# Second-half values turned by the DMA crossbar instead of TensorE, and a fixed table for the units between the feed-forward steps

## The chip, the cores and the metric

The kernel runs on one core of one Trainium2 chip. The metric is the device time of one execution in microseconds (us). A trace of the hardware profiler goes with one execution of each kernel; its span runs from the first to the last recorded instruction and is 1.7 to 2.2 us shorter than the device time, which matters below. Kernels of one job ran on the same chip, in turn with the kernel before.

## The reference

Attention with block-sorted keys and values, then a bilinear feed-forward layer. Cut to what matters:

```python
B, H, S, D = 4, 8, 768, 64;  n_blocks = 8          # blocks of 96 positions
P = sort_net                                        # (B, H, 8, 8), five rounds of
                                                    # exp and row and column normalisation
k_sorted = einsum('bhij,bhjcd->bhicd', P, k_blocks) # mix blocks of k, and of v
v_sorted = einsum('bhij,bhjcd->bhicd', P, v_blocks)
attn = softmax(q_blocks @ k_sorted^T / 8)           # within each block of 96
x = (attn @ v_sorted), heads side by side           # (3072, 512)
out = ((x @ w_a) * (x @ w_b)) @ w_out               # w_a, w_b: 512x1536, w_out: 1536x512
```

## The kernel before

(PSUM, in what follows, is the memory into which TensorE writes its results; a semaphore is a counter on which an engine or a transfer queue waits; the DMA crossbar is what transposes a tile while a DMA transfer moves it.)

Everything is computed with heads in pairs (hp = 0 to 3 in the first batch). The first batch is the special one: nothing is there yet to hide its attention behind, so its positions are split into two halves of four blocks. The first half's attention runs ahead of all feed-forward work; the second half's is cut into units that stand between the twelve feed-forward steps of the first half.

The units that the change touches (cut):

```python
def half_scores(h, hp):              # "sc": scores of four blocks, then the exponential on ScalarE
    ...
    nc.scalar.activation(out=eT[:, 0, :, 0:HB], in_=sc[0:BLK, :, 0:HB], func=AF.Exp, ...)

def half_v(h, hp):                   # "vs_ps": v of four blocks turned by TensorE, copied by VectorE
    g = h * HP + hp
    vT, vs = vTs[hp], vss[g % NBUF]  # three buffers for turned v
    vs_ps = psF.tile([P, NBH, 2, D], BF16, tag="F", name="vs_ps")
    for i in range(NBH):
        nc.tensor.matmul(vs_ps[:, i], lhsT=vT[:, h * NBH + i], rhs=ident, is_transpose=True)
    nc.vector.tensor_copy(out=vs[0:BLK, 0:NBH, V0:V0 + P], in_=...vs_ps...)

def half_o(h, hp):                   # "o_ps": probabilities times v; reciprocal and scaling on VectorE
    ...
def half_x(h, hp, eng):              # "xt_ps": result turned by TensorE and copied into xT
    ...
```

and their order:

```python
def units_half():
    def R(hp):
        half_scores(1, hp)
        half_v(1, hp)
    us = []
    for hp in range(HP):
        us.append(lambda hp=hp: R(hp))
        if hp > 0:
            us.append(lambda hp=hp: half_x(1, hp - 1, "dve"))
        us.append(lambda hp=hp: half_o(1, hp))
    us.append(lambda: half_x(1, HP - 1, "dve"))
    return us

interleave(steps, units_half(), 1, 2)   # evenly: from the third step on, the last step alone
```

A step (`ffn_ab`) is eight matmuls of 128x384 into two PSUM tiles; steps are numbered from 0 to 11. GpSimd's queue loads k, v, q and the weights, in six chunks of w_a and w_b each; a chunk serves two steps. Later batches already have v turned by the crossbar (`return_v`).

The softmax here doesn't subtract the row's maximum and nothing guards it: scores larger than these inputs give would overflow.

Of the kernel before, what the change touches and what calls it, by code (L numbers as in the profile page):

```python
# [16 lines left out]
def _ap(t: bass.AP, extra_offset, pattern):  # L17
    return bass.AP(tensor=t.tensor, offset=t.offset + extra_offset,
                   ap=[list(p) for p in pattern])
# [3 lines left out]
def kernel(  # L23
# [11 lines left out]
    nc = tc.nc  # L35
    P = 128
# [10 lines left out]
    HP = H // 2  # L47
    KA = DMODEL // P
    KO = DFF // P
    NBH = NB // 2  # L50
# [4 lines left out]
    V0 = 16  # L55
# [18 lines left out]
    ident = const.tile([P, P], BF16, name="ident")  # L74
# [50 lines left out]
    NBUF = 3  # L125
    kTs = [const.tile([P, S + PAD], BF16, name=f"kT{n}") for n in range(HP)]
    vTs = [const.tile([P, NB, P], BF16, name=f"vT{n}") for n in range(HP)]
    eTs = [const.tile([BLK, 2, 2, HB + PAD], BF16, name=f"eT{n}") for n in range(NBUF)]
    vss = [const.tile([P, NB, VW], BF16, name=f"vs{n}") for n in range(NBUF)]
# [13 lines left out]
    def xT_of(b):  # L143
        if b not in xTs:
            xTs[b] = xtp.tile([P, KA, S], BF16, tag="xT", name="xT")
        return xTs[b]
# [12 lines left out]
    def copy(eng, out, in_):  # L159
        if eng == "act":  # L160
            nc.scalar.copy(out=out, in_=in_)  # L161
        else:
            nc.vector.tensor_copy(out=out, in_=in_)  # L163

    def keep_busy(ps, n, cols=512):
        for _ in range(n):
            nc.tensor.matmul(ps[:, 0:cols], lhsT=warm[:, 0:P], rhs=warm[:, 0:cols],  # L167
                             start=True, stop=True)


    def mix_mms(g, what, where):
        src2 = loaded[g][0 if what == "k" else 1]
        for c in range(NCH):
            for e in range(2):
                nc.tensor.matmul(where(c)[e * D:(e + 1) * D], lhsT=src2[:, e, c * D:(c + 1) * D],  # L175
                                 rhs=s_all[:, 2 * g + e], start=True, stop=True)

    def mix_first(g, what, engines, fill=0, cols=512):
        mix = [psF.tile([P, 512], FP32, tag="F", name="mixf") for _ in range(2)]
        keep_busy(mix[0], fill, cols)  # L180
        mix_mms(g, what, lambda c: mix[c // 3][:, c % 3 * P:(c % 3 + 1) * P])
        for u, eng in enumerate(engines):
            copy(eng, turned(g, what, u),
                 _ap(mix[u], 0, [[512, P], [P, 3], [CG, NB], [1, CG]]))

    def turned(g, what, u):
        if what == "k":
            return _ap(kTs[g % HP], u * 3 * CG, [[S + PAD, P], [CG, 3], [BLK, NB], [1, CG]])
        return _ap(vTs[g % HP], u * 3 * CG, [[NB * P, P], [CG, 3], [P, NB], [1, CG]])

    def half_scores(h, hp):
        g = h * HP + hp
        kT, qT, eT = kTs[hp], st[hp, "qT"], eTs[g % NBUF]
        sc = psA.tile([P, 2, 512], FP32, tag="A", name="sc")
        for i in range(NBH):
            for e in range(2):
                nc.tensor.matmul(  # L197
                    sc[:, e, i * BLK:(i + 1) * BLK],
                    lhsT=kT[e * D:(e + 1) * D, (h * NBH + i) * BLK:(h * NBH + i) * BLK + P],
                    rhs=qT[e * D:(e + 1) * D, :, (h * NBH + i) * CG:(h * NBH + i + 1) * CG],  # L200
                    start=True, stop=True)
        nc.scalar.activation(out=eT[:, 0, :, 0:HB], in_=sc[0:BLK, :, 0:HB],  # L202
                             func=AF.Exp, scale=float(scale))

    def half_v(h, hp):
        g = h * HP + hp
        vT, vs = vTs[hp], vss[g % NBUF]
        vs_ps = psF.tile([P, NBH, 2, D], BF16, tag="F", name="vs_ps")
        for i in range(NBH):
            nc.tensor.matmul(vs_ps[:, i], lhsT=vT[:, h * NBH + i], rhs=ident, is_transpose=True)  # L210
        nc.vector.tensor_copy(out=vs[0:BLK, 0:NBH, V0:V0 + P],
                              in_=vs_ps[0:BLK].rearrange("p i e d -> p i (e d)"))

    def half_o(h, hp):
        g = h * HP + hp
        xp = att.tile([BLK, NBH, 2, D], BF16, tag="xph", name="xph")
        one_o(eTs[g % NBUF], 0, vss[g % NBUF], 0, xp, NBH)
        st["x", h, hp] = xp

    def half_x(h, hp, eng):  # L220
        xT, xp = xT_of(0), st["x", h, hp]
        xt_ps = psF.tile([P, NBH, BLK], BF16, tag="F", name="xt_ps")
        for i in range(NBH):
            nc.tensor.matmul(xt_ps[:, i, :], lhsT=xp[:, i],  # L224
                             rhs=ident[0:BLK, 0:BLK], is_transpose=True)
        copy(eng, xT[:, hp, h * HW:(h + 1) * HW].rearrange("p (i t) -> p i t", i=NBH), xt_ps)

    def one_o(eT, hf, vs, i0, xp, nxp):
        rec = att.tile([BLK, 2, NBH], FP32, tag="rec", name="rec")
        o_ps = psA.tile([P, 2, 512], FP32, tag="A", name="o_ps")  # L230
        for i in range(NBH):
            for e in range(2):
                nc.tensor.matmul(o_ps[:, e, i * (D + 1):(i + 1) * (D + 1)],  # L233
                                 lhsT=eT[:, hf, e, i * BLK:i * BLK + P],
                                 rhs=vs[0:BLK, i0 + i, V0 - 1 + e * (D + 1):V0 + D + e * (D + 1)],
                                 start=True, stop=True)
        nc.vector.reciprocal(
            out=rec, in_=_ap(o_ps, 0, [[1024, BLK], [512 + D, 2], [D + 1, NBH]]))
        nc.vector.tensor_tensor(  # L239
            out=_ap(xp, i0 * 2 * D, [[nxp * 2 * D, BLK], [D, 2], [2 * D, NBH], [1, D]]),  # L240
            in0=_ap(o_ps, 1, [[1024, BLK], [511, 2], [D + 1, NBH], [1, D]]),
            in1=_ap(rec, 0, [[2 * NBH, BLK], [NBH, 2], [1, NBH], [0, D]]),
            op=ALU.mult)
# [180 lines left out]
    with tc.manual_schedule(engines={ET.PE, ET.Pool, ET.SP}):  # L424
        with tc.manual_schedule(engines={ET.Activation, ET.DVE}):
# [7 lines left out]
            for it in range(5):  # L433
# [8 lines left out]
                if it == 2:  # L442
                    with nc.allow_low_precision("sum of one one and zeros"):
                        nc.vector.reduce_sum(
                            out=mask, in_=_ap(ident, 0, [[P, P], [1, CG], [CG, NB]]),
# [14 lines left out]
                else:  # L460
                    nc.vector.tensor_mul(
                        out=p_fin.bitcast(BF16).rearrange("h (i j u) -> h i j u", i=NB, j=NB),
# [30 lines left out]
            def partial(n, *kcs):  # L493
                if n not in begun:
                    begun[n] = (psF.tile([P, 512], FP32, tag="F", name="pf") if n < 3 else
                                psA.tile([P, 2, 512], FP32, tag="A", name="two")[:, 0])
                ab_mms(begun[n], (w_a_sb, w_b_sb)[n % 2], 0, n // 2, 0, kcs)
# [3 lines left out]
            mix_first(1, "v", ("act", "dve"), 1)  # L501
            mix_first(1, "k", ("act", "dve"))
            half_scores(0, 0)
            half_v(0, 0)
            mix_first(2, "v", ("act", "dve"))
            mix_first(2, "k", ("act", "act"))
            half_o(0, 0)
            half_scores(0, 1)
            half_v(0, 1)
            half_v(0, 2)  # L510
            mix_first(3, "k", ("dve", "act"))
            half_scores(0, 2)
            half_o(0, 1)
            mix_first(3, "v", ("act", "act"))
            half_x(0, 0, "dve")
            half_o(0, 2)
            half_x(0, 1, "act")
            half_scores(0, 3)
            partial(0, 0)
            half_v(0, 3)  # L520
            partial(0, 1)
            half_x(0, 2, "dve")
            half_o(0, 3)
            partial(4, 0, 1, 2)
            partial(2, 0, 1, 2)
            partial(0, 2)
# [18 lines left out]


        def units_half():
            def R(hp):
                half_scores(1, hp)
                half_v(1, hp)  # L550

            us = []
            for hp in range(HP):
                us.append(lambda hp=hp: R(hp))
                if hp > 0:
                    us.append(lambda hp=hp: half_x(1, hp - 1, "dve"))
                us.append(lambda hp=hp: half_o(1, hp))
            us.append(lambda: half_x(1, HP - 1, "dve"))
            return us

# [48 lines left out]
        for n, (b, u, g) in enumerate(seq):  # L609
            if u is c_ and plain(g):  # L610
                late = 3 if g % HP == 0 else 2
                after[n + 1] += [lambda g=g, what=what: in_order(g, what) for what in "kv"]
                if late == 3:
                    after[n + 3].append(lambda g=g: nc.gpsimd.tensor_copy(
                        out=gate, in_=xT_of(g // HP - 1)[0:1, HP - 1, 0:1]))
# [8 lines left out]
        units = [[] for _ in range(B)]  # L624
        for (b, u, g), then in zip(seq, after):
            units[b].append(lambda u=u, g=g, then=then: unit(u, g, then))

        def interleave(steps, units, spare, first):
            n, done = len(steps) - spare - first, 0
            for s, step in enumerate(steps):  # L630
                step()
                want = -(-(s + 1 - first) * len(units) // n)
                while done < min(want, len(units)):
                    units[done]()
                    done += 1

        def paced(ab, po, units, spare, last):
            steps = ab + po
# [2 lines left out]
            for now, step in enumerate(steps, 1):  # L641
# [4 lines left out]
                if now == len(steps) - 1 and last:  # L646
                    units[main]()

        steps = [lambda: ffn_ab(0, 0, 0, begun[0:2]), lambda: ffn_ab(0, 1, 0, begun[2:4]),
                 lambda: ffn_ab(0, 2, 0, begun[4:5])]  # L650
        steps += [lambda m=m: ffn_ab(0, m, 0) for m in range(3, KO)]
        interleave(steps, units_half(), 1, 2)

        for b in range(B):
            ab = [lambda m=m, t=t, b=b: ffn_ab(b, m, t)
# [33 lines left out]
```

## Time and profile before

| | kernel before |
|---|---|
| time, median of 6 fast runs of the first job | 242.24 us (241.85 to 242.38) |
| span of the trace | 240.8 us |
| TensorE busy, of the span | 97% |
| stretch from the first scores of the second half (25.87) to the last step of the first half (41.44) | 15.57 us |
| longest wait of TensorE in it, for the exponential | 0.63 us |

"Stretch" means this in all that follows: on the chain of work that ended last, from the start of the second half's first scores to the start of the pieces of step 11 (drawn there as 2.60 us of `pf`, step 11 merged with the first step of the second half). It takes in all of the changed units and is free of the scatter of the prologue, whose end varies by some 0.7 us from trace to trace (25.20 to 25.87). The lines of the profile are shown in the prediction.

### The profile page before, as it was taken

Reading aid. Unit: us, or ns where it says so; the run is one execution under the profiler, and the core shown is the slowest. Engines: PE = TensorE matmul, PEld = TensorE weight load, DVE = VectorE, ACT = ScalarE, POOL = GpSimd, SP = SyncE. Lnnn points to the kernel's source line nnn. Section 1 sums busy time; section 2 is a strip of 40 time slices with the busy share of each in tenths; the row PEclk is TensorE's granted clock in tenths of the full one; section 3 lists DMA queues with packets and bytes.
Section 4 is the critical chain, followed back from the end, with each engine's and each line's share of the span. In section 5 each row is a group of like instructions: output and inputs, shape, how many; then the busy total and the mean of one; then the engine's idle time right before and its main releaser. Section 6 shows DMA issues by size and latency. Waiting matters only on the chain.

```text
span 240.8 us, 5193 instructions
## 1 busy us (share of the span) xinstructions
PE 234.4 (97%) x2091; PEld 139.5 (58%) x2091; DVE 111.3 (46%) x262; ACT 101.1 (42%) x187; POOL 70.4 (29%) x97
## 2 busy tenths in 40 slices
PE   7999899999999999999999999999999999999994
PEld 7776566666554466666645455666544566665443
DVE  6688657546435234465406234544544144344110
ACT  3675543665630175744640356455510133333001
POOL 8777569623220045070602516131000000000000
PEclk9999999999999999999999999999999999999999
DMA  5999999995999569869997897981415200000132
GB/s 77 203 198 196 197 200 201 203 160 90 147 157 203 133 110 150 131 100 196 140 142 197 151 227 129 124 171 36 76 57 143 95 36 3 0 0 3 44 130 88
DMA packets 63527, 30.35 MB, mean 126 GB/s; under 512 B 40336, under 2 KB 60560, under 8 KB 63504
## 3 DMA queue, kind: packets, MB, share of 16 engines
q0 software_dynamic: 20944, 14.16, 42.8%
q1 hardware_dynamic: 42416, 15.81, 34.1%
q8 instruction: 16, 0.26, 0.4%
q10 hardware_dynamic: 144, 0.07, 0.1%
q14 instruction: 7, 0.06, 0.1%
HBM read 28.32 MB, written 6.29 MB: 144 GB/s over the span
## 4 chain that ended last, share of the span: by engine, by line
PE 93%; DVE 3%; ACT 1%; DMA 1%; issue 0%; DVEq 0%; ACTq 0%
PE pf L357 52%; PE po L402 24%; PE o_ps L233 3%; PE sc L327 2%; PE mix L175 2%; PE mix L298 2%; PE mixf L175 1%; PE po L387 1%; PE sc L197 1%; PE vs_ps L210 1%; PE heat L167 1%; PE xt_ps L224 1%; DMA p_nat<-in_sort_net_dram 1%; PE q_ps L262 1%; PE two L357 1%; DVE xp L239 1%
## 5 line engine op out<-in xcount | busy, mean ns | idle before, releaser
L378 DVE TENSOR_TENSOR hT<-a_sb,pf 128x384 bf16<-128x384 bf16 x95 | 52.6, 553 | 71.6 <-PE pf L357 45.2
L357 PE MATMUL pf<-xT,w_a_sb 128*128 128x384 bf16 x380 | 77.9, 326 | 0.0
L357 PE MATMUL pf<-xT,w_b_sb 128*128 128x384 bf16 x380 | 77.4, 326 | 0.0
L377 ACT CAST a_sb<-pf 128x384 bf16<-128x384 f32 x95 | 45.4, 479 | 63.3 <-PE pf L357 39.9
L402 PE MATMUL po<-w_out_sb,hT 128*128 128x512 bf16 x276 | 61.9, 379 | 0.0
L357 PEld LDWEIGHTS <-w_b_sb 128*128 128x128 bf16 x384 | 37.5, 98 | 24.7
L357 PEld LDWEIGHTS <-w_a_sb 128*128 128x128 bf16 x384 | 35.3, 98 | 22.4
L402 PEld LDWEIGHTS <-hT 128*128 128x128 bf16 x276 | 26.3, 98 | 30.1
L161 ACT COPY o_sb<-po 128x512 f32<-128x512 f32 (+1 forms) x13 | 7.5, 577 | 48.9 <-PE po L402 47.5
L163 DVE COPY o_sb<-po 128x512 f32<-128x512 f32 (+1 forms) x12 | 7.9, 658 | 38.7 <-PE po L402 34.1
L332 ACT ACTIVATE eT<-sc 96x768 bf16<-96x768 f32 x24 | 18.0, 802 | 5.2 <-PE sc L327 5.2
L239 DVE TENSOR_TENSOR xp<-o_ps,rec 96x512 bf16<-96x512 f32 x24 | 15.9, 684 | 0.3
L314 POOL COPY kT<-turned 128x768 bf16<-128x768 bf16 x6 | 5.0, 826 | 35.0 <-DMA turned<-nat 26.7
L233 PEld LDWEIGHTS <-eT 96*128 96x128 bf16 x256 | 10.2, 97 | 4.4 <-ACT eT L202 1.1
L96 POOL DMA_DIRECT2D k<-in_k_dram x16 | 11.6, 724 | 3.6 <-PE pf L357 1.3
L96 POOL DMA_DIRECT2D v<-in_v_dram x16 | 11.5, 721 | 2.8 <-DMA w_b_sb<-in_moe_w_b_dram 1.3
L233 PE MATMUL o_ps<-vs,eT 96*128 96x65 bf16 x256 | 11.4, 193 | 1.0 <-ACT eT L202 0.6
L577 POOL COPY gate<-kT 1x1 bf16<-1x1 bf16 x4 | 0.7, 178 | 32.8 <-ACT kT L280 28.3
L161 ACT CAST nat<-mix 128x768 bf16<-128x768 f32 (+1 forms) x12 | 7.7, 638 | 4.2 <-PE mix L298 3.5
L167 PE MATMUL heat<-warm 128*128 128x128 bf16 x84 | 8.0, 272 | 1.3 <-DVE warm L77 1.3
L248 POOL COPY qc<-q 128x768 bf16<-128x768 bf16 x10 | 8.4, 844 | 2.6 <-DMA q<-in_q_dram 2.6
L96 POOL DMA_DIRECT2D q<-in_q_dram x12 | 8.7, 722 | 1.5 <-DMA w_a_sb<-in_moe_w_a_dram 0.6
(86 smaller groups left out, 164.6 us busy)
## 6 DMA issues: line engine op xcount, KB each, us to landing
out_dram<-o_sb SPq DMA_DIRECT2D x17, 256.0 KB, 2.0
k<-in_k_dram POOLq DMA_DIRECT2D x16, 192.0 KB, 5.8
v<-in_v_dram POOLq DMA_DIRECT2D x16, 192.0 KB, 6.9
q<-in_q_dram POOLq DMA_DIRECT2D x12, 192.0 KB, 7.0
w_a_sb<-in_moe_w_a_dram POOLq DMA_DIRECT2D x6, 256.0 KB, 8.6
w_b_sb<-in_moe_w_b_dram POOLq DMA_DIRECT2D x6, 256.0 KB, 9.2
w_out_sb<-in_moe_w_out_dram POOLq DMA_DIRECT2D x3, 512.0 KB, 12.3
out_dram<-o_sb SPq DMA_DIRECT2D x12, 128.0 KB, 2.4
```

The costliest lines, as they stand in the source:

```text
L96: nc.gpsimd.dma_start(out=to, in_=_ap(t, base, [[W, P], [S * D, 2], [1, W]]))
L161: nc.scalar.copy(out=out, in_=in_)
L163: nc.vector.tensor_copy(out=out, in_=in_)
L167: nc.tensor.matmul(ps[:, 0:cols], lhsT=warm[:, 0:P], rhs=warm[:, 0:cols], start=True, stop=True)
L233: nc.tensor.matmul(o_ps[:, e, i * (D + 1):(i + 1) * (D + 1)], lhsT=eT[:, hf, e, i * BLK:i * BLK + P], rhs=vs[0:BLK, i0 + i, V0 - 1 + e * ( ...
L239: nc.vector.tensor_tensor(out=_ap(xp, i0 * 2 * D, [[nxp * 2 * D, BLK], [D, 2], [2 * D, NBH], [1, D]]), in0=_ap(o_ps, 1, [[1024, BLK], [511 ...
L248: nc.gpsimd.tensor_copy(out=qc.rearrange("p c e d -> p e c d"), in_=loaded[g][2].rearrange("p e (c d) -> p e c d", c=NCH))
L332: nc.scalar.activation(out=eT[:, hf, :, 0:HB], in_=sc[0:BLK, :, 0:HB], func=AF.Exp, scale=float(scale))
L357: nc.tensor.matmul(pf[:, 0:HW], lhsT=w_sb[:, kc, m * P:(m + 1) * P], rhs=x_cols(b, kc, t), start=(kc == 0), stop=(kc == KA - 1))
L377: nc.scalar.copy(out=a_sb, in_=pf[:, 0:HW])
L378: nc.vector.tensor_mul(out=hT[:, m, t * HW:(t + 1) * HW], in0=a_sb, in1=ab[1][:, 0:HW])
L402: nc.tensor.matmul(held["po"], lhsT=hTs[b][:, m, c * P:(c + 1) * P], rhs=w_out_sb[:, m, :], start=(m == 0), stop=(m == KO - 1))
```

## The change

Its intent: take four groups of transposes and four VectorE copies off the engines by letting the DMA crossbar turn (transpose) v of the second half straight into its buffer, early, while the first half is still under way; and take scores one unit ahead of the outputs, by a fixed table, so that no output waits for an exponential.

```diff
+    def second_v(hp):
+        nc.sync.dma_start_transpose(out=vss[(HP + hp) % NBUF][:, 0:NBH, V0:V0 + P],
+                                    in_=vTs[hp][:, NBH:].rearrange("p i t -> p (i t)"))
 ...
             half_o(0, 1)
+            second_v(0)
 ...
             half_o(0, 2)
+            second_v(1)
 ...
             half_o(0, 3)
+            second_v(2)
 ...
         def units_half():
-            def R(hp):
-                half_scores(1, hp)
-                half_v(1, hp)
+            def O(hp):
+                half_o(1, hp)
+                if hp == 0:
+                    second_v(HP - 1)
-            us = []
+            us = [lambda: half_scores(1, 0)]
             for hp in range(HP):
-                us.append(lambda hp=hp: R(hp))
+                if hp + 1 < HP:
+                    us.append(lambda hp=hp: half_scores(1, hp + 1))
                 if hp > 0:
                     us.append(lambda hp=hp: half_x(1, hp - 1, "dve"))
-                us.append(lambda hp=hp: half_o(1, hp))
+                us.append(lambda hp=hp: O(hp))
 ...
-        interleave(steps, units_half(), 1, 2)
+        interleave(steps, units_half(), (0, 0, 1, 1, 2, 1, 2, 1, 1, 2, 1, 0))
```

Each transpose can start only when the last output that reads its buffer has gone: the fourth waits for the second half's own first output.

More of the change, by code (lines that the diff above doesn't have):

```diff
@@ L203, in half_scores, with half_v @@
                              func=AF.Exp, scale=float(scale))
-    def half_v(h, hp):
-        g = h * HP + hp
-        vT, vs = vTs[hp], vss[g % NBUF]
+    def second_v(hp):
+        nc.sync.dma_start_transpose(out=vss[(HP + hp) % NBUF][:, 0:NBH, V0:V0 + P],
+                                    in_=vTs[hp][:, NBH:].rearrange("p i t -> p (i t)"))
+    def half_v(hp):
+        vT, vs = vTs[hp], vss[hp % NBUF]
         vs_ps = psF.tile([P, NBH, 2, D], BF16, tag="F", name="vs_ps")
         for i in range(NBH):
-            nc.tensor.matmul(vs_ps[:, i], lhsT=vT[:, h * NBH + i], rhs=ident, is_transpose=True)
+            nc.tensor.matmul(vs_ps[:, i], lhsT=vT[:, i], rhs=ident, is_transpose=True)
         nc.vector.tensor_copy(out=vs[0:BLK, 0:NBH, V0:V0 + P],
@@ L503 @@
             half_scores(0, 0)
-            half_v(0, 0)
+            half_v(0)
             mix_first(2, "v", ("act", "dve"))
@@ L508 @@
             half_scores(0, 1)
-            half_v(0, 1)
-            half_v(0, 2)
+            half_v(1)
+            half_v(2)
             mix_first(3, "k", ("dve", "act"))
@@ L519 @@
             partial(0, 0)
-            half_v(0, 3)
+            half_v(3)
             partial(0, 1)
@@ L626, with interleave @@
             units[b].append(lambda u=u, g=g, then=then: unit(u, g, then))
-        def interleave(steps, units, spare, first):
-            n, done = len(steps) - spare - first, 0
-            for s, step in enumerate(steps):
+        def interleave(steps, units, counts):
+            todo = iter(units)
+            for step, n in zip(steps, counts):
                 step()
-                want = -(-(s + 1 - first) * len(units) // n)
-                while done < min(want, len(units)):
-                    units[done]()
-                    done += 1
+                for _ in range(n):
+                    next(todo)()
         def paced(ab, po, units, spare, last):
```

## The prediction

> **What bounds the kernel now.** I read the page first: the busy shares, then the 40 slices, then the chain that ended last. After those I looked only at the stretch that the change touches.
>
> ```profile
> PE 234.4 (97%) x2091; PEld 139.5 (58%) x2091; DVE 111.3 (46%) x262; ACT 101.1 (42%) x187; POOL 70.4 (29%) x97
> ...
> PE   7999899999999999999999999999999999999994
> ...
> PEclk9999999999999999999999999999999999999999
> DMA  5999999995999569869997897981415200000132
> ...
> PE 93%; DVE 3%; ACT 1%; DMA 1%; issue 0%; DVEq 0%; ACTq 0%
> ```
>
> TensorE is busy in 97% of the span at full clock, and 93% of the chain is TensorE. So a microsecond taken from TensorE's work, or from a wait of it, is a microsecond of the time, unless it turns into another wait. In the 40 slices the DMA row matters too: slices 2 to 9 (about 6 to 54 us) are at 9, the loads of weights, k, v and q. The four transposes that the change adds must run in just that stretch.
>
> The stretch concerned is feed-forward steps 3 to 11 of the first batch's first half, with the second half's attention placed between them. The chain of waits over it, in order of time (start us, us, what):
>
> ```profile
> 25.87 0.36 PE sc L197 x8
> ...
> 26.32 0.81 ACT eT L202
> 27.13 0.05 issue
> 27.18 0.42 PE o_ps L233 x8
> 27.60 1.30 PE pf L357 x8
> 28.90 0.28 PE sc L197 x8
> 29.18 0.33 PE vs_ps L210 x4
> 29.51 1.30 PE pf L357 x8
> 30.81 0.17 PE xt_ps L224 x4
> 30.98 1.30 PE pf L357 x8
> 32.28 0.25 PE o_ps L233 x8
> ```
>
> The reader sees the price list. A step is 1.30 us, scores (sc) 0.28, the transposes of v (vs_ps) 0.33, an output unit (o_ps) 0.25, the transposes of x (xt_ps) 0.17. At 26.3 TensorE waits for ScalarE's exponential, since the scores and the output of the first pair stand side by side. The timeline shows both the wait and what the copy costs VectorE:
>
> ```profile
> 26.15 0.40 PE L210 MATMUL vs_ps<-ident,vT 128*128 128x128 bf16 x4
> ...
> 26.59 0.42 DVE L211 COPY vs<-vs_ps 96x512 bf16<-96x512 bf16 x1
> ...
> 27.18 0.42 PE L233 MATMUL o_ps<-vs,eT 96*128 96x65 bf16 x8 [0.63 <-ACT eT L202]
> ```
>
> **What the Trainium skill says.** (1) "VectorE: DVE Perf Modes", section "The three transpose paths": a 128x128 bf16 transpose is given as 390 ns on TensorE, into PSUM, and 1309 ns by the DMA crossbar, into SBUF. Alone, the crossbar is slower; it pays only as it runs beside TensorE. The trace shows less on TensorE: 222 ns each in the groups of this stretch, and 0.33 us for four, as they overlap. (2) "Advanced Engine Details and Errata", section "X-Bar Transpose (TRN2)": transposing DMAs are as fast as regular ones. For throughput the trace agrees: from 54.5 to 55.5 us, with only transposes under way, 877 packets (0.22 MB) moved in 1 us, while the loads alone move 0.20 MB per us. (3) "DMA: Bandwidth & Descriptors", section "Rules for kernel authors": queues of all issuing engines run on the same 16 DMA engines and interleave, and a transpose beside ordinary DMAs needs no ordering. The trace agrees, and shows the cost, which the page does not give. In the only transpose of before that meets the full load (qTf, issued at 42.7 us):
>
> ```profile
> q0 software_dynamic: 631, 0.63, 92.0%
> q1 hardware_dynamic: 605, 0.15, 28.9%
> ...
> qTf<-qc SPq DMA_TRANSPOSE x1, 10.5
> ```
>
> The first two lines are of 46.5 to 50.5 us: packets alternate about one to one, and the loads fall from 0.20 to 0.16 MB per us. The third: 10.5 us from issue to landing, against 2.7 us for the one at 53.7 us on idle engines.
>
> **The change, part by part.**
> *Removed from TensorE.* Four times four transposes. Three stand on the chain at 0.33 us: 0.99 us. The first lies within the wait for the exponential, so it counts there.
> *Removed wait.* Between the end of the first scores (26.15, where vs_ps starts) and the output unit (27.18) 1.03 us pass, the first vs_ps among them. With the table, scores of pair 0 come after step 2, scores of pair 1 after step 3, the output of pair 0 after step 4. Two steps (2.6 us) lie between the exponential's cause and its use, against the 0.81 us that it takes. The 1.03 us go.
> Sum: 2.0 us. Check from the other side: steps 3 to 11 are 9 x 1.30 = 11.70, four of each unit 4 x (0.28 + 0.25 + 0.17) = 2.80, together 14.5 us; in before they last from 25.87 to 42.57 (the first step of the next half), 16.7 us. That gives 2.2, the difference being drain times. I take 2.0.
> *Removed from VectorE.* Four copies of 0.42 us, 1.7 us. It is 46% busy, so this is worth nothing directly; it frees PSUM buffers a little.
> *New, small waits.* The table puts the x unit of pair 2 and the output of pair 3 both after step 9. Summing the prices, step 9 ends at 37.2. VectorE then has the product of step 9 (0.55), the copy of x (0.35), the reciprocal (0.20) and the scaling (0.69) before x of pair 3 can start: 37.4 + 1.8 = 39.2, while step 10 ends at 38.9. A wait of 0.3; and some 0.1 for x of pair 2. Cost 0.4 us.
> *Added transposes, latency.* Each moves 128x512 bf16, 128 KB in 256-byte packets: 512 packets. From the qTf above: nothing for 3.8 us (42.7 to 46.5), then 150 packets per us, then about 1.3 us to the landing. For 512 packets beside load packets of 512 to 768 bytes the alternation is faster (0.20 MB per us by 0.77 to 1.0 KB per pair gives 195 to 260 pairs per us), so 2.0 to 2.6 us, and 7 to 8 us in all. The first three are let go by the outputs of the first half, at 19.0, 20.0 and 22.0 us by the timeline, so they land at about 26, 28 and 30. Their outputs by my sums stand at 29.0, 32.3 and 35.6 us. No wait. The fourth needs the buffer that the first output reads, so it is issued at 29.4 and lands at 36.4 to 37.4; its use is at 37.35. This is the tight one: I put 0.3 us on it.
> *Added transposes, load on the loads.* 128 KB at 0.20 MB per us is 0.65 us of delay each, 1.9 us by the time three are through, 2.6 in all. The tile views of w_a and w_b give issue and landing: chunk 1 lands at 20.9 and 22.3, the last at 31.6 and 33.0, one each 1.33 us. The tightest is w_b's chunk 2, due 24.9, with up to 2 us more 26.9, wanted in the middle of step 4 at 28.4. Chunk 3: 27.7 + 2 against 31.7. No wait, but only 1.5 us to spare. k and v of the next pairs and w_out have over 3 us.
>
> Net: 2.0 - 0.4 - 0.3 = 1.3 us, and since TensorE bounds the rest and its later work is paced by its own steps, it should reach the end whole. 242.2 - 1.3 = 240.9; the removed copies and 14.5 instead of 14.7 pull slightly the other way. I say 240.8 us.
>
> **The rivals.**
> (a) The crossbar comes late: the fourth transpose takes the full 10.5 us of qTf, lands at 39.9, and TensorE waits 2.5 us before the last output. That eats the gain and more: about 242.7. For it speaks the only sample under full load; against it that this sample has 1.5 times the packets and larger load packets in its way.
> (b) The loads are pushed back more than their share, a weight chunk comes late in step 4 or 6, and TensorE waits there by 1 us or more: about 241.5 to 242.5. For it speaks the saturated DMA row; against it that the total rate stayed at 0.20 MB per us when both kinds ran together, so only bytes are lost, not efficiency.
> (c) All is hidden, and the two small waits on VectorE do not appear, as the copies are gone: the full 2.2 us, 240.0.
> (d) The removed transposes were hidden, as 97% busy is not peak. Against it: in the chain each adds a full 0.33 us between the scores and the next step. It would leave the 0.7 us of the exponential: 241.5.
>
> **Range and chances.** (c) gives the low end, with a little for run-to-run spread (0.4 us in before): 239.9. (a), weighed at perhaps one in six, sits just above the high end, which I set at 242.0. A change by 2% would need 4.8 us; at most 2.2 us are to be had, and a loss of 4.8 us would need a transpose to take over 14 us. So faster 0.01, same 0.98, slower 0.01.
>
> **What would show each step right or wrong.** Right: the vs_ps transposes of four in the first 42 us fall from 32 instructions to 16; no wait for the exponential after step 2; the first step of the second half begins near 40.9 instead of 42.57; transposes of v issued at 19 to 29 us land in 6 to 9 us. Wrong: a TensorE wait for a DMA of vs ahead of the last output unit (a), or for w_a or w_b in steps 4 to 10 (b); or a gain in this stretch that is lost again after 45 us, at the first q or k units or w_out, which I hold unlikely.

## The result, and the profile after

| | before | changed | |
|---|---|---|---|
| first job, median | 242.24 us | 241.31 us | ratio 0.9963 (0.9949 to 0.9976) |
| second job, another set of rounds | 242.16 us | 241.11 us | ratio 0.9968 (0.9948 to 0.9988) |
| stretch, in the traces | 15.57 us | 13.94 us | -1.63 us |

A ratio is the mean time of one kernel's fast runs over that of the other's of the same rounds, so not quite the ratio of the medians that stand beside it. One of the changed kernel's six runs in the first job was slow (251.53 us) and is left out.

The page of the changed kernel: the busy line, the row of the DMA engines in 40 slices, the chain by engine.

```profile
PE 233.4 (98%) x2075; PEld 138.7 (58%) x2075; DVE 109.6 (46%) x258; ACT 100.7 (42%) x187; POOL 70.4 (29%) x97
...
DMA  5999999999998489679996899970434300000132
...
PE 95%; DVE 3%; ACT 1%; issue 0%; DVEq 0%
```

Sixteen TensorE instructions fewer, 1.0 us less busy, and the chain is TensorE's to 95% instead of 93%: the bound is what it was. The chain over the stretch, in order of time (start us, us, what):

```profile
25.80 0.35 PE sc L197 x8
26.14 1.41 PE pf L360 x8
27.55 0.28 PE sc L197 x8
27.82 1.41 PE pf L360 x8
29.23 0.25 PE o_ps L236 x8
...
37.59 0.34 PE xt_ps L227 x4
37.93 0.25 PE o_ps L236 x8
38.18 1.30 PE pf L360 x8
39.48 0.26 PE xt_ps L227 x4
39.74 2.60 PE pf L360 x16
```

The `vs_ps` pieces and the wait for the exponential are gone. New is the 1.41: a step costs 0.11 us more where it follows scores directly. In the kernel before such a step followed the transposes and cost 1.30, so of their 0.33 us only 0.22 were theirs; the other 0.11 belong to the changeover after the scores and stay. (The kernel with the crossbar alone, below, bears this out: an x unit that stands right behind scores takes 0.28 us there instead of 0.17.) At 37.59 and 39.48 the x units take 0.17 and 0.09 us over their price of 0.17; on the timeline their weight loads wait 0.39 and 0.30 us for VectorE's scaling (`xph`).

The account of the stretch: three pieces of `vs_ps` gone, -0.99; from the first scores to the first output or step, 0.35 instead of 1.31, -0.96; the first output at its price, -0.17; four steps of 1.41 instead of 1.30, +0.44; x units 0.94 instead of 0.85, +0.09. Sum -1.59, against -1.63 read directly.

From there to the last TensorE piece nothing differs: 41.44 to the end of the last TensorE piece at 237.68 before, 39.74 to 235.98 after, 196.24 us in both. So 1.63 us reached the end of TensorE's work whole. But the time is only 0.9 to 1.05 us less. The rest went after the end of all TensorE work, which the closing waits of the transfer queue show (waited for: us in total, times, longest), first before, then changed:

```profile
SPq L684 <- DMA out_dram<-o_sb: 1.5, 2, 1.3
```

```profile
SPq L690 <- DMA out_dram<-o_sb: 1.7, 1, 1.7
```

Before, the program's end waits twice for stores, 1.5 us in all; afterwards once, 1.7 us. The trace's single records tell why. The transfers of this queue take eight semaphores in turn, the last store (issued by ScalarE) among them. At the end SyncE waits for each of the eight in a fixed order, 0.06 us apiece when there is nothing to wait for. The last store lands 2.01 us after the last TensorE instruction in both kernels. Before, its semaphore was the fifth of the eight, so the first four were ticked off before it landed and three remained; the four new transfers move it to the first place, and seven remain.

| after the last TensorE instruction, us | before | changed |
|---|---|---|
| last store lands | 2.01 | 2.01 |
| closing waits passed after that landing | 4 (from 2.03) | 8 (from 2.02) |
| end of the span | 3.09 | 3.37 |

That is +0.28 us. Another +0.3 us lies outside the span: time minus span is 1.72 to 1.83 us in all runs of the kernel before and 2.05 to 2.16 in all of the changed one, on both chips. So -1.63 + 0.28 + 0.33 = -1.02, which the second job's -1.05 bears out.

The transfers, in the view of the DMA queues from 23 to 31 us of the trace, first before, then changed (each row of digits is 40 slices of 0.2 us):

```profile
DMA  9999999999999999999999999999999999999999
...
q0 software_dynamic: 3131, 1.55, 144.5%
```

```profile
DMA  9999999999999999999900199999999999999999
...
q0 software_dynamic: 1892, 0.94, 91.8%
q1 hardware_dynamic: 1632, 0.39, 48.2%
```

The loads move 0.61 MB less, the transposes 0.39 MB: 0.22 MB are lost altogether. Most of it is a hole of some 0.7 us, near 27 us, in which the engines move next to nothing. The same view of two more kernels with these transposes (crossbar alone, one store moved) has it too; those without them (the kernel before and the changed one without v) have not. The transposes of v land 6.9, 8.7, 9.1 and 6.9 us after their issue, at 25.8, 29.0, 31.2 and 36.4 us; the outputs that need them stand at 29.23, 32.63, 36.04 and 37.93. For the weights, the tile view of w_b of the changed kernel (in that of the kernel before, the line ends in 6.6/9.2/10.4):

```profile
DMA to landing us min/median/max: 6.7/11.0/14.5
```

w_b's fourth chunk (two chunks before the last) lands at 31.25 us instead of 27.7, and is first used at 31.82 by the timeline: nothing waits, but 0.6 us are left; with the landing of the kernel before it would be 4.1. In the traces of four later kernels with the same start (changed again, fourth late, one store moved, product early) w_b's third and fourth chunks land only 0.2 to 0.7 us ahead of their use.

### The profile page after: what moved, and what is told of

Its sections match the earlier page's. It is cut to its first block, busy times and chain, and to the rows that moved or that the text cites. A ratio compares the mean times of both kernels' runs of the same rounds, so it can differ in the third digit from the quotient of the medians.

```text
span 239.3 us, 5178 instructions
## 1 busy us (share of the span) xinstructions
PE 233.4 (98%) x2075; PEld 138.7 (58%) x2075; DVE 109.6 (46%) x258; ACT 100.7 (42%) x187; POOL 70.4 (29%) x97
## 4 chain that ended last, share of the span: by engine, by line
PE 95%; DVE 3%; ACT 1%; issue 0%; DVEq 0%
PE pf L360 52%; PE po L405 24%; PE o_ps L236 3%; PE sc L330 2%; PE heat L167 2%; PE mix L175 2%; PE mix L301 2%; PE mixf L175 1%; PE po L390 1%; PE sc L197 1%; PE xt_ps L227 1%; PE q_ps L265 1%; PE two L360 1%; DVE xp L242 1%; PE vs_ps L213 0%; DVE o_sb L163 0%
```

## The experiments

Twelve runs were made, one of them the changed kernel again. "Stretch" is read from each trace as above. Tail is from the last TensorE instruction to the end of the span; outside is time minus span, over all runs.

| kernel | time, median us | ratio to before | stretch | tail | outside |
|---|---|---|---|---|---|
| before (three jobs) | 242.04, 242.16, 242.22 | 1 | 15.57 | 3.09 | 1.72 to 1.83 |
| changed, second time | 241.11 | 0.9968 | 13.95 | 3.34 | 2.06 to 2.16 |
| table alone | 241.24 | 0.9967 | 14.84 | 3.09 | 1.74 to 1.79 |
| crossbar alone | 241.90 | 0.9988 | 14.89 | 3.36 | 1.85 to 1.96 |
| both transpose | 242.47 | 1.0024 | 15.56 | 3.36 | 1.87 to 1.93 |
| changed, no v at all | 240.43 | 0.9939 | 13.95 | 3.10 | 1.73 to 1.83 |
| fourth late | 240.89 | 0.9955 | 13.96 | 3.36 | 2.06 to 2.12 |
| one store moved | 240.28 (fast runs) | 0.9924 | 13.95 | 2.91 | 1.87 to 1.94 |
| x later | 240.31 (fast runs) | 0.9938 | slow trace, see there | 2.94 | 1.74 to 1.84 |
| table alone, one count | 241.34 | 0.9965 | 14.85 | 2.92 | 1.74 to 1.82 |
| product early | 239.97 (fast runs) | 0.9935 | 13.69 | 2.94 | 1.73 to 1.81 |
| weights late | 247.06 | 1.0195 | stalls | 3.36 | 2.07 to 2.11 |
| one more by crossbar | 247.91 | 1.0231 | stalls later | 2.92 | 1.72 to 1.82 |

### The table alone

```diff
-            us = []
+            us = [lambda: R(0)]
             for hp in range(HP):
-                us.append(lambda hp=hp: R(hp))
+                if hp + 1 < HP:
+                    us.append(lambda hp=hp: R(hp + 1))
-        interleave(steps, units_half(), 1, 2)
+        interleave(steps, units_half(), (0, 0, 1, 1, 2, 1, 2, 1, 1, 2, 1, 0))
```

> The kernel before, with its units of the second half (each scores unit still followed by its four transposes of v on TensorE) spread by the changed kernel's table. Theory A (the gain is the sum of a removed wait for the exponential, about 0.6 us, and of TensorE's transposes, about 0.22 us each): the 0.63 us wait ahead of the first output of the second half is gone, the stretch up to the second half's first step is 0.5 to 0.7 us shorter, time about 241.6. Rival B (nearly all of the gain is the table, the crossbar adds nothing): time about 241.3, as the changed kernel. Rival C (the table only keeps the crossbar from stalling): time 242.2, as before.

Chain of the stretch's beginning:

```profile
25.96 0.33 PE vs_ps L210 x4
26.29 1.30 PE pf L357 x8
```

The wait is gone, the transposes stay, the steps cost 1.30: -0.73 us in the stretch. Tail and outside are those of the kernel before, and the time fell by 0.8 us, as much as with the whole change. By the time alone rival B had won. By the chain it had not: the changed kernel's stretch is 0.9 us shorter still.

### The crossbar alone

The changed kernel with the units of the kernel before, each output right behind its scores after step 2:

```diff
-            us = [lambda: half_scores(1, 0)]
+            us = []
             for hp in range(HP):
-                if hp + 1 < HP:
-                    us.append(lambda hp=hp: half_scores(1, hp + 1))
+                us.append(lambda hp=hp: half_scores(1, hp))
-        interleave(steps, units_half(), (0, 0, 1, 1, 2, 1, 2, 1, 1, 2, 1, 0))
+        interleave(steps, units_half(), 1, 2)   # as in the kernel before
```

> The changed kernel, with the units of the second half spread as in the kernel before. Theory A: the transposes of pairs 1 to 3 are gone from TensorE's path, 3 x 0.22 = 0.66 us; that of pair 0 lay inside the wait for the exponential, which stays and becomes about 0.85 us long; time about 241.6. Rival B: 242.2. Rival C: 241.3.

```profile
26.23 0.82 ACT eT L202
...
27.09 0.42 PE o_ps L236 x8
...
28.81 0.28 PE sc L197 x8
29.09 1.41 PE pf L360 x8
```

The wait ahead of the first output is 0.96 us now instead of 0.63, since the transposes that filled part of it are gone. The stretch is 0.68 us shorter, as Theory A has it. The two halves alone give -0.73 and -0.68; together they give -1.63, 0.22 more than the sum, and that is the first pair's transposes, which cost nothing as long as the wait covers them. But tail and outside give back 0.27 and 0.1 us, and of the 0.66 expected only 0.3 were left by the ratio, whose interval (0.9970 to 1.0006) doesn't exclude no gain: in the time, the crossbar's gain isn't shown by this run.

### Both transpose

The kernel before with `second_v` at the changed kernel's four places, while TensorE turns v as before and overwrites the result.

```diff
             half_o(0, 1)
+            second_v(0)     # and likewise after the outputs of pairs 2, 3 and the second half's first
```

> The kernel before, with the four crossbar transposes added at the places of the changed kernel while TensorE still turns v and overwrites what they wrote (result stays right). It measures what the transposes cost by themselves. Theory A: the loads have room, so TensorE's chain is as before to 0.2 us and the time is 242.2 to 242.4. Rival D (the transposes cost time outside the chain, which is why 1.6 us less in the trace's stretch came out as only 0.9 us less time): the span is as before, the time 0.4 us or more longer. Rival of the late load: a wait of TensorE for w_a or w_b in steps 4 to 8, time 243 or more.

The stretch is as before to 0.01 us, tail +0.27, outside +0.1: 0.4 us slower by the medians, at the edge of the noise (1.0000 to 1.0048). This is the cost of four transfers more, with nothing gained: it lies wholly after TensorE's end. Rival D is right about the place for 0.4 us; that of the late load is out here.

### The changed program without v

```diff
     def second_v(hp):
-        nc.sync.dma_start_transpose(...)
+        pass
```

> The changed kernel without its four crossbar transposes: the second half uses stale values of v, so the result is wrong on purpose. It gives the time of the changed TensorE program without any load on the DMA engines. Theory A: the transposes are hidden, the time is as the changed kernel's, 241.2 to 241.4. Rival D: 240.8 or less. The landings of the weight chunks should be those of the kernel before (w_b's third at 27.7 us instead of 31.3).

Its output is wrong, which doesn't matter for the time. The stretch is the changed kernel's to 0.01 us, so the crossbar's transposes are hidden from TensorE entirely. Rival D has the time right: it is 0.7 us under the changed kernel's in the second job. Tail (0.25) and outside (0.3) explain most of it; the rest is within what two jobs differ by. The chunks land as in the kernel before, w_b's fourth (the expectation's "third") at 27.7.

### The fourth transpose, let go later

```diff
-                if hp == 0:
+                if hp == 1:
                     second_v(HP - 1)
```

> The changed kernel with the fourth crossbar transpose let go one output unit later (after the second output instead of the first), into the same buffer. It is then issued at about 32.9 us instead of 29.5. If landing takes 6.9 us or more under the load as in the changed kernel, it lands at 39.8 to 41, TensorE waits 1.9 to 3 us ahead of the last output (now at 37.9), and the time is 243.2 to 244.3: the transposes' latency is hidden by placement, with 1.5 us to spare in the changed kernel. Rival (the latency is set by the loads' end and is shorter later): no wait, 241.3.

Nothing changed: the transpose was issued at 29.1 us and landed at 35.8. The queue's wait is for the last reader of its buffer, the first output, wherever the call stands in the program, and the queue had nothing else to do. So this run did not test what it was made for; it is a repetition of the changed kernel, and the margin of the fourth transpose (1.5 us by the trace) was not tried.

### One store moved to GpSimd's queue

```diff
-            nc.sync.dma_start(out=rows[c], in_=o_sb)
+            queue = nc.gpsimd if b == B - 1 and c < 1 else nc.sync
+            queue.dma_start(out=rows[c], in_=o_sb)
```

beside which the changed kernel itself was run again.

> The changed kernel itself again, in the same rounds as the next ones and on one chip with them. Theory E, from the first four runs: between the last TensorE instruction and the end of the span the kernels with the four added transposes take 3.36 us and those without them 3.09, as the queue's closing waits go over eight DMA semaphores in a fixed order, and four more transfers shift which of them belongs to the last store, so that seven waits of 0.06 us follow the landing instead of three. Expected: time about 0.9 us under the kernel before again, tail 3.36 us. Time minus span was 2.05 to 2.15 in the first job, 1.85 to 1.95 for the two other kernels with the transposes and 1.72 to 1.83 without: here 1.85 to 2.15 if that belongs to the transposes, 1.8 if it was the chip of the first job.

> The changed kernel with one store of the last batch issued by GpSimd, so that the last store falls on the semaphore that is waited for last. Theory E: the chain up to the last TensorE instruction stays, the tail falls from 3.36 to about 2.9 us (seven waits of 0.06 us fewer), time 0.4 to 0.45 us under the changed kernel of these rounds. Rival (the tail belongs to the transposes themselves): tail 3.36, same time.

The changed kernel came out as in the first job. With one transfer less on the queue the last store's semaphore is the last of the eight; seven of the closing waits pass before it lands, one after. The same view of closing waits:

```profile
SPq L692 <- DMA out_dram<-o_sb: 1.3, 2, 1.1
```

The tail fell from 3.34 to 2.91 us with the chain above it unchanged, so it is the count of transfers and not the transposes that made it long. The time fell by 0.8 us, more than the 0.43 of the tail; outside fell by 0.2 too, for a reason that no run shows. Two of its six runs were slow (246.1 and 246.4).

### The table alone with the last store on the same semaphore

The table alone, with five stores moved (`c < 5`), so that its last store too is waited for last.

> The table alone (transposes of v stay on TensorE), with five stores of the last batch issued by GpSimd, so that here too the last store falls on the semaphore waited for last. The fair partner of the kernel with the crossbar and one store moved (240.3 us, chain 15.57 - 1.63 = 13.94 us in the stretch, tail 2.91). Expected: stretch 14.84, tail 2.9, time 0.2 us under the table alone, so about 241.1: the crossbar is then worth 0.8 to 0.9 us, which the changed kernel's tail and the part outside the span hid. Rival (the crossbar is worth nothing): 240.3.

Stretch 14.85, tail 2.92: as expected. The time, 241.34 by the median and 0.9965 by the ratio, is not better than the table alone in its own job (0.9967); 0.2 us is within the noise of these jobs. The fair comparison stands: 0.9965 against 0.9924 for the kernel with the crossbar and one store moved, 0.41% or 1.0 us. The traces give 0.90 of it in the stretch.

### The table once more

x of pair 2 moved behind step 10 and copied by ScalarE, on top of the store moved:

```diff
-            # order and table, in short: s, o and x with the pair's number
-            return [... o2, x2, o3, x3], counts (0, 0, 1, 1, 2, 1, 2, 1, 1, 2, 1, 0)
+            return [... o2, o3, x2, x3], counts (0, 0, 1, 1, 2, 1, 2, 1, 1, 1, 2, 0)
```

> The one before, with the table changed: x of pair 2 after step 10 and copied by ScalarE, the last output alone after step 9. The changed kernel waits 0.17 us for VectorE ahead of x of pair 2 and 0.09 ahead of x of pair 3. Expected: both gone, 0.2 to 0.3 us less than the one before; if the copies then come late for the next half's first step, nothing.

Three of seven runs were slow (244.3 to 249.8), the profiled one among them; the fast runs are at 240.2 to 241.2. Up to 42 us the slow trace is undisturbed: by the timeline 13.53 us lie between the first scores and step 11, as many as in the next form. What made this one run long came later: TensorE waits 0.82 us for GpSimd's product (until 42.91) and 5.33 us for a v turned by the crossbar (until 78.50), and from 76.8 us on the granted clock is 0.50 for 6.8 us. Why the transfers were late in this execution is not shown.

### GpSimd's product early

The same, and GpSimd's product for the next batch moved ahead of the loads:

```diff
         for c in range(4, 6):
             load_ab(c)
+        spread(nc.gpsimd, p_col, 8, 8)
         for hp in range(3):
             load_pair(1, hp)
-        spread(nc.gpsimd, p_col, 8, 8)
```

> The kernel with the table changed for x of pair 2 and one store moved, with GpSimd's product for the second batch's first pairs (s_all) put ahead of the loads of k, v, q. In the changed kernel it ends at 41.0 us, 1.8 ahead of its use; in the kernel before at 37.0, 7.4 ahead. Expected: no change of the fast runs except that both small waits of VectorE (0.17 and 0.09 us) are gone from the chain: 240.0 to 240.2. If the slow runs of that kernel (3 of 7) came through this product alone they should become fewer; if through the loads as a whole, not.

```profile
36.99 0.25 PE o_ps L237 x8
37.24 1.30 PE pf L361 x8
38.54 0.35 PE xt_ps L228 x8
38.89 2.60 PE pf L361 x16
```

Both x units now stand together at 0.35 us with no wait: stretch 13.69, 0.25 us less. Three of the five fast runs are at 239.85 to 239.97, the lowest of all kernels here, but two are at 241.1 and 241.6 and a sixth was slow (243.6), so the interval (0.9911 to 0.9960) does not set it apart from the kernel with one store moved (0.9911 to 0.9937). Both beat the kernel before; the latter is also clear of the changed kernel (0.9948 to 0.9988). Whether the early product makes slow runs rarer, one in six against three in seven does not say.

### The weights three loads later

```diff
             load_ab(2)
+            load_pair(1, 0)
             load_ab(3)
 ...
-        for hp in range(3):
+        for hp in range(1, 3):
             load_pair(1, hp)
```

> The changed kernel with the k, v, q of one pair loaded ahead of the fourth weight chunks, which come some 3 us later by that. In the changed kernel that chunk of w_b lands at 31.25 us, 0.7 us ahead of its use; in the kernel before it lands at 27.7, 4 us ahead. If the transposes used up the loads' room, TensorE now waits 2 to 2.5 us in step 6 and the time is 243 to 244. If the loads have room (the prediction put the chunk at 29.6): no wait or under 0.5 us, 241.2 to 241.7.

TensorE waits 1.92 us for w_a and 0.77 us for w_b in step 6, 2.7 us in all: the room was used up, as expected. (No run has the late weights without the crossbar's transposes. An estimate: w_b lands at 34.56 here, 3.3 us later than in the changed kernel; 3.3 us after the 27.7 of the kernel before would be 31.0, still ahead of 31.8.) But the time is 5.9 us over the changed kernel's 241.1. The table of stretches of this trace (window, length, busy us of each engine, granted clock, DMA share, GB/s):

```profile
31.00:33.00 2.00, 0.08 (x2) 0.08 (x2) 0.76 (x2) 0.00 (x0) 0.76 (x2) 1.00 1.46 195
33.00:34.60 1.60, 0.83 (x4) 0.23 (x5) 0.00 (x0) 0.48 (x1) 0.70 (x1) 0.67 1.36 186
...
39.00:40.00 1.00, 1.00 (x7) 0.62 (x6) 0.28 (x1) 0.00 (x0) 1.00 (x1) 0.50 1.33 201
```

By the shares of these windows and their neighbours the granted clock is 0.50 from about 33.5 to 40.4 us. It falls 0.6 us after the first wait has ended (32.92) and before the second begins (33.83). So TensorE works at half speed for some 6.1 us of these 6.8, which by estimate costs another 3.0; with the waits that is 5.7 of the 5.9. A late load was thus priced at less than half of what it costs.

### One more v by the crossbar

On top of the early product: `return_v` for the second batch's first pair too, in place of its eight TensorE transposes.

```diff
-                if g > HP:
+                if g >= HP:
                     return_v(g)
-            if g == HP:
-                turn_v(g)
```

> The same, and v of the second batch's first pair turned by the crossbar too instead of TensorE (eight transposes, about 0.45 us of the chain), the count of queue transfers kept. The added transfer is 256 KB and meets the loads of w_out: issued at 44, it lands at 55 to 57 by the times of before, and it is used at 56.3. If it lands in time: 239.7. If it lands late or holds back the q turned behind it: 240.5 to 243.

TensorE's timeline, the waits in brackets:

```profile
56.02 0.67 PE L237 MATMUL o_ps<-vs,eT 96*128 96x65 bf16 x16 [0.82 <-DMA vs<-vT]
61.29 0.52 PE L331 MATMUL sc<-qTf,kT 64*128 64x96 bf16 x16 [2.00 <-DMA qTf<-qc]
```

It landed 12.1 us after its issue, 0.8 too late, and worse, every transpose behind it on the queue was pushed back: q's came after 14.5 us. There are five waits for transposes, 7.1 us in all, and the clock drops to 0.50 after the longest of them (2.53 us). The same means that paid in the changed kernel makes it 2.3% slower than the kernel before one step further, and 3.0% slower than the kernel that it was built on (1.0231 against 0.9935).

## Why the prediction was right, point by point

The prediction said 240.8 us (239.9 to 242.0), a change of under 2%, for the reason that TensorE bounds the kernel and the change takes work and a wait from it. The measured time is 241.3 and 241.1, and the parts alone show the reason in the stretch: -0.73 from the table, -0.68 from the crossbar, -1.63 together. By the time alone the changed kernel is no faster than the table alone (0.9967); it is the pair with equal tails, 0.9965 against 0.9924, that shows the crossbar's share there. The signs that it named came too: 16 `vs_ps` transposes fewer, and the second half's first step at 40.88 us by the timeline (40.9 forecast).

*Removed from TensorE, 0.33 us each.* Direction right, size off: 0.22. The 0.11 between is the changeover from scores to a step, which the chain had charged to the transposes since they stood between.

*Removed wait, 1.03 us.* Right: 0.96 are gone between the first scores and what follows, and another 0.17 at the first output, which had started from an idle engine.

*New waits on VectorE, 0.4 us.* Too large: 0.26 us over the price of the two x units, and 0.17 of these had been there before at x of pair 3. The net is 0.09, and the larger wait came at x of pair 2, not of pair 3. That the waits are of the kind named is shown by the last table, which removed them.

*Latency of the transposes.* Right to about 1 us: 25.8, 29.0, 31.2 and 36.4 us against the 26, 28, 30 and 36.4 to 37.4 that the prediction worked out from one sample. The 0.3 us put on the fourth did not come. (One reading was off: the transpose of 2.7 us did not run on idle engines, as w_out's last load landed at 54.45 us and another transpose was under way until 55.65.)

*Load on the loads.* The mechanism was right, the size not: 3.6 us of delay at w_b's fourth chunk instead of 1.9, as rival (b)'s counter-argument, that only bytes are lost, failed. Near 27 us both queues stand still for 0.7 us. No wait came of it, but at the fourth chunk 0.6 us were left, where the prediction's sum leaves 2.0. At the third, which it called the tightest with 1.5 to spare, it was 2.5 in the first trace and 0.3 to 0.7 in the four later ones. The experiment with later weights shows the edge.

*Reaching the end whole.* This step failed. The stretch gave 1.63 us, more than the 1.3 predicted net, and all of it reached the last TensorE instruction. Then 0.28 us were lost in closing waits whose number hangs on the count of transfers, and 0.3 us outside the span. The prediction looked only as far as TensorE's end. The two errors partly cancel, so the predicted net of 1.4 us (242.2 to 240.8) stands against 0.9 to 1.05 measured. That the number came so close is in part luck: inside the stretch, too, the transposes priced 0.33 us too high in all stand against 0.6 us set aside for waits that did not come.

*Rivals.* (a) did not occur: the fourth transpose took 6.9 us and not 10.5; the run meant to try its margin did not. (b) did not occur, with 0.2 to 0.7 us to spare in the traces. (c) did not occur: both small waits appeared, and the stretch gave 1.63 us and not 2.2. (d) is refuted by the crossbar alone, where the stretch is shorter by just the transposes of three pairs.

What stays open: what makes up the time outside the span. It is 1.7 to 1.85 us in seven of the thirteen programs, 1.85 to 1.96 in three and 2.05 to 2.16 in the changed one and its near copies; three programs with the transposes are in the lowest group, so it is not the transposes as such. Also open is why slow runs came in four kernels with the transposes (7 of 55 runs of all kernels with them, none in the 24 of the other five) and in none of 56 runs of kernels without them, counting the 39 of the kernel before. A shrunken margin of the loads would fit. The one slow trace shows late transfers and the lower clock, but not what made them late, and no run was made that shows it.

## What to carry to other kernels

A piece of a chain is worth its price only if what follows does not rise when it is taken away, so compare the neighbours' durations with and without it before multiplying. Work moved to a busy transfer queue takes the room of other transfers: look for the tightest landing, not for the mean, and remember that a wait on it can cost more than it lasts. And when the last engine's work ends as early as predicted but the time does not, look at the tail: the count of transfers alone moved it by 0.43 us here.

## What the Trainium skill lacked or had wrong

- "DMA: Bandwidth & Descriptors", section "DMA Transpose (X-bar)": nothing on latency beside other loads. Here 128 KB landed after 6.9 to 9.1 us under full load, 256 KB after 12.1, while in the kernel before 192 KB issued at 53.7 us, as the last load was about to land (54.45), took 2.7.
- "Advanced Engine Details and Errata", section "X-Bar Transpose (TRN2)": transposing DMAs as fast as regular ones. For transposes alone the traces agree; mixed with loads from GpSimd's queue the engines moved 1.33 MB in 8 us instead of 1.55, with a hole of 0.7 us in which nearly nothing moved.
- "TensorE: Matmul & The Clock Gate", section "HAM oscillation — how this bites in real kernels": the rule is no idle gaps over some 3.4 us. Here the clock was at 0.50 from 0.6 us after the end of a wait of 1.92 us, for 6.8 us, while in another run a wait of 2.00 us left it at 1.00.
- No page has the closing waits: eight semaphores of the transfer queue, 0.06 us each, in a fixed order. Where the last store's semaphore stands among them is worth up to 0.46 us (tail 2.91 to 3.37).
- No page has the size of the 0.11 us that a step of 128-row matmuls costs more right behind scores of 64 rows (1.41 against 1.30). "TensorEngine Tiling (Array Packing)", section "Key Properties", says that changing the tiling mode drains TensorE, without a figure; whether that is what is seen here no run shows.
